# Attention pairs of one kind handled in joint steps, with the conversion of the first MLP's weights moved on the clock

## The chip, the cores and the metric

The kernel runs on one core of a Trainium2 chip. A core has five engines with instruction queues of their own, each worked off in order: PE (TensorE, matmuls), DVE (VectorE), ACT (ScalarE), POOL (GpSimd) and SP (SyncE, which issues the DMAs here). The metric is the device time of one execution in microseconds (us). Before the change it is 902.57 us, the median of three runs (900.73 to 903.84).

## The reference

Attention over 4 batches, 8 heads, 576 positions and a head width of 64, in fp32, then two MLPs over the 2304 tokens:

```python
scores = scale * np.matmul(q, k.transpose(0, 1, 3, 2))
mask_local = (rel >= 0) & (rel < 32)
mask_strided = (rel >= 0) & (pos[None, :] % 32 == pos[:, None] % 32)
scores = np.where(masks[None], scores, -1e9)      # heads 0-3 local, heads 4-7 strided
attn = np.exp(scores - scores.max(-1)); attn /= attn.sum(-1) + 1e-9
x = np.matmul(attn, v)                             # to (2304, 512)
h = x @ w_in;  x = (h * np.cos(h)) @ w_out         # 512 -> 2048 -> 512
g = x @ w_gate; x = (g * sigmoid(g) * (x @ w_val)) @ w_out2   # 512 -> 1536 -> 512
```

The kernel takes q, k, v and the results in float32 and the weights in float64, whose words it converts on the chip.

## The kernel before

**Attention (lines 321 to 455 and 622 to 709).** Two heads share the 128 partitions as a pair: 4 batches by 4 pairs, of which two are local (windows of 64 queries by 96 keys) and two strided (the positions of one residue modulo 32 stand together, three residues to a block of 54 by 54). A pair is cut into three groups of three local or four (last three) strided tiles. One step k of the loop at line 661 starts one group of a strided pair and the same group of a local pair, so that 8 runs of two pairs by 3 groups make 24 steps. A group is worked on over six steps: masks and scores on PE and the row maxima on DVE in its own step, exponentials on ACT one step later, row sums and a reciprocal on DVE and the division on POOL (`norm`, line 408) two steps later (LAGS[0]), transposes on PE and their copies out of PSUM on ACT three steps later, the product with v on PE four steps later, and the store into the token tile on ACT (`put`, line 442) five steps later. Each of these is one instruction (or a few) per group, so twice per step. Buffers turn: 4 score or scratch banks of PSUM, 2 transposed banks, 2 output banks, 3 tiles of q and k and of v per kind.

**The loads.** SP issues them in program order: q and k of a run (`load_qk`, 592 or 594 KB a pair), v (432 KB local, 2 by 162 KB strided), and 512 KB chunks of the weights (`load_raw`, six buffers). A chunk's buffer is loaded again as soon as the DVE instruction that reads it last has been issued. On POOL, `scale_q` multiplies the q of the next run by 1/8 in each middle group's step; it waits for that run's load.

**The filler.** Work on the weights is a queue of small pieces, each with a cost in us of DVE time (`later`, line 176). `pump(share)` adds a credit and takes pieces until it is spent; it is called twice in an attention step, with PUMP = 1.0 from step KP = 4 on. In order: for each of the 16 chunks of w_in a conversion to fp32 (`conv_steps`, line 197: ACT line 221, DVE lines 224, 228 and 232: scan for the maximum, shift, combine); from chunk XSAT = 12 on also the scale and the fp16 split of the first token block (lines 457 to 480); the common scale of w_in (lines 114 to 135); then for each chunk the split into two fp16 parts (`split_chain`, line 260: ACT line 242, DVE line 245), with the scan of one chunk of w_out (line 171) behind each. `need(key)` takes pieces until the one with that key is done, whatever the credit.

**First MLP (lines 833 to 889).** 80 slots: 5 token blocks by 16 hidden tiles. In a slot PE does the up projection of one tile (12 matmuls of up to 512 columns, line 503, "up1"), DVE, ACT and POOL make h*cos(h) of earlier tiles (DVE lines 519 and 526: two instructions a slot), and from slot HEAD = 14 on PE also does the down projections of tiles whose turn it is, as many as keep the queue of finished tiles at the length `lag`, which falls from HEAD - 2 to 2 by RATE = 0.4 a slot. Slot 0 is run inside the attention loop, at step 25, behind `need(("in", 0))`; the rest follow after step 29. The second load, conversion and split of w_out (`direct_later`, line 291) is filler again, and a down projection of tile m first takes pieces until w_out's chunk m is split. A PSUM bank of an up projection is free when DVE's second instruction has read it; up to slot HEAD - 5 every second projection uses one of four further banks. The weights of the second MLP are scanned, converted and written out behind that, with budgets of HSHARE, SHARE and SHARE2 of the DVE time that PE's work leaves.

Of the kernel before, what the change touches and what calls it, by code (L numbers as in the profile page):

```python
# [51 lines left out]
PUMP, KP = 1.0, 4  # L52
XSAT = 12
EARLY, K0 = 1, 1
HEAD, HSHARE = 14, 0.8
# [5 lines left out]
SHARE, SHARE2, SB = 0.95, 0.7, 2  # L61
# [14 lines left out]
def build(tc, qk_l, qk_s, v_l, v_s, w_in, w_out, w_gate, w_val, w_out2, mask_l, mask_s, eye32, eye16, out):  # L76
    nc = tc.nc
    wide = w_in.dtype != F32
    with ExitStack() as ctx:
# [117 lines left out]
        def conv_steps(mat, j, dst, scan, free=load_raw):  # L197
# [38 lines left out]
            return box, [(0, g0)] + [(0.63, g1)] * scan + [(0.36, g2), (0.63, g3)]  # L236
# [20 lines left out]
        def chain_later(mat, j, tiles):  # L257
            begin(conv_steps(mat, j, lambda: as_f32(tiles[j + 2]), True)[1])
# [65 lines left out]
        pa = attn.enter_context(tc.tile_pool(name="pa", bufs=2, space=bass.MemoryType.PSUM))  # L324
# [15 lines left out]

        units = [(b, p) for b in range(NB) for p in (2, 0, 3, 1)]
        qk_t, v_t = {}, {}

        def load_qk(i):
            b, p = units[i]
            loc = is_local(p)
            qk_t[i] = ap.tile([128, QKW[loc]], F32, name="qkl" if loc else "qks", bufs=3)
            nc.sync.dma_start(out=qk_t[i], in_=(qk_l if loc else qk_s)[b, p % 2])

        def load_v(i):  # L350
            b, p = units[i]
            loc = is_local(p)
            if loc:
                v_t[i] = ap.tile([LW, LT, 128], F32, name="vl", bufs=3)
                nc.sync.dma_start(out=v_t[i], in_=v_l[b, p % 2])
            else:
                v_t[i] = v_pair[i // 2 % 3]
                for u in range(2):
                    nc.sync.dma_start(out=v_t[i][64 * u:64 * u + SW, SP * u:SP * u + SP, :], in_=v_s[b, p % 2, u])
# [4 lines left out]
        def scale_q(i):  # L364
            q = qk_t[i][:, 0:S if is_local(units[i][1]) else QP]
            nc.gpsimd.tensor_scalar(out=q, in0=q, scalar1=SCALE, scalar2=1.0, op0=ALU.mult, op1=ALU.mult)

        class Group:
            def __init__(self, i, g):
                self.i, self.g = i, g  # L370
                self.b, self.p = units[i]
                self.loc = is_local(self.p)
                self.i0, self.n = groups(self.p)[g]
                self.w = LW if self.loc else SW

            def mask(self):
                n, w = self.n, self.w
                b = bank()
                self.sc = b[:, 0:n * w].rearrange("p (n w) -> p n w", w=w)
                mask = (ml[:, 0:3] if self.g == 0 else ml[:, 1:4]) if self.loc else ms[:, 0:n]  # L380
                nc.tensor.matmul(out=self.sc, lhsT=id16, rhs=mask, start=True, stop=False)
                nc.tensor.matmul(out=b[:, 288:512], lhsT=ones16, rhs=hot[:, 0:224], start=False, stop=False)

            def scores(self):
                for i in range(self.n):
                    q0 = (64 if self.loc else SW) * (self.i0 + i)
                    k0 = (S if self.loc else QP) + q0
                    for h in range(2):
                        r = slice(64 * h, 64 * h + 64)
                        nc.tensor.matmul(out=self.sc[r, i, :], lhsT=qk_t[self.i][r, q0:q0 + 64],  # L390
                                         rhs=qk_t[self.i][r, k0:k0 + self.w], start=False, stop=i == self.n - 1)

            def top(self):
                self.mx = ap.tile([128, 4], F32, name="mx", bufs=3)
                m = self.mx[:, 0:self.n]
                nc.vector.tensor_reduce(out=m, in_=self.sc, op=ALU.max, axis=AX.X, negate=True)

            def exps(self):
                self.t = (e_l if self.loc else e_s)[(self.i // 2 * 3 + self.g) % 4]
                self.e = self.t[:, 0:self.n, 0:self.w]  # L400
                for i in range(self.n):
                    nc.scalar.activation(out=self.e[:, i, :], in_=self.sc[:, i, :], func=AF.Exp, bias=self.mx[:, i:i + 1])

            def sums(self, ls):
                self.ls = ls
                nc.vector.tensor_reduce(out=self.ls[:, 0:self.n], in_=self.t[:, 0:self.n, 0:self.w + 1], op=ALU.add, axis=AX.X)

            def norm(self):
                nc.gpsimd.tensor_tensor(out=self.e, in0=self.e,
                                        in1=self.ls[:, 0:self.n].unsqueeze(2).to_broadcast([128, self.n, self.w]), op=ALU.mult)  # L410

            def transposes(self):
                if self.loc:
                    self.tp = pa.tile([128, self.n, 128], F32, name="tp")[0:LW]
                    for i in range(self.n):
# [237 lines left out]
        for i in range(2):  # L653
            scale_q(i)
# [419 lines left out]
```

## Time and profile before

| | |
|---|---|
| median of three runs | 902.57 us |
| profiled execution, its own time | 901.94 us |
| its span (first to last instruction) | 900.2 us |
| busy: PE, DVE, ACT, POOL | 857.6, 607.9, 490.9, 184.5 us |
| moved by DMA | 150.94 MB |

PE is busy for 95% of the span, but this is a mean over very different stretches. The profile's second part, 40 slices of 22.5 us, shows PE at six to eight tenths in the first five slices, with the DMA engines at nine tenths in the first three, and at nine tenths from there on. The attention loop and slot 0 take the first 122 us; what is left is nearly unbroken matmul work. Busy time of an engine is a sum over its instructions; what a stretch is limited by is read from what ends the idle time before them.

### The profile page before, as it was taken

The numbers are of one execution on the slowest core, as the hardware profiler recorded it, in microseconds if no ns is written. First come the engines' busy times: TensorE is split into PE (matmuls) and PEld (weight loads), VectorE is DVE, ScalarE is ACT, GpSimd is POOL, SyncE is SP. The second block draws the span as 40 slices with busy tenths as digits, with TensorE's granted clock in tenths as the row PEclk, the third lists the DMA queues.
The fourth block names the chain that finished last, engine by engine and source line by source line (L and its number), as shares of the span: only waits on it lengthen the run. The fifth ranks groups of instructions, "written<-read, shape, count | busy, mean of one in ns | idle before, by whom it ended". The sixth has DMA issues, their size and how long they took to land.

```text
span 900.2 us, 16865 instructions
## 1 busy us (share of the span) xinstructions
PE 857.6 (95%) x6687; PEld 561.1 (62%) x6687; DVE 607.9 (68%) x1138; ACT 490.9 (55%) x974; POOL 184.5 (20%) x223
## 2 busy tenths in 40 slices
PE   7678799999999999999999999999999999999997
PEld 5557544444444444555556777777777777888885
DVE  6678979887658989986687456554544554565444
ACT  4678878763435777654677334443434443443433
POOL 3344414212215666532222100000000000000000
PEclk9798999999999999999999999999999999999999
DMA  9998762357544565554243343343425334544501
GB/s 275 336 286 257 227 234 70 118 187 253 196 171 170 192 216 183 187 201 127 71 153 135 122 155 118 129 149 144 165 91 202 112 135 151 202 180 170 201 1 36
DMA packets 35391, 150.94 MB, mean 168 GB/s; under 512 B 4240, under 2 KB 5520, under 8 KB 31472
## 3 DMA queue, kind: packets, MB, share of 16 engines
q1 hardware_dynamic: 35312, 149.87, 48.9%
q8 instruction: 52, 0.85, 0.4%
q14 instruction: 27, 0.22, 0.1%
HBM read 134.13 MB, written 15.73 MB: 166 GB/s over the span
## 4 chain that ended last, share of the span: by engine, by line
PE 74%; DVE 10%; DMA 6%; ACT 4%; issue 3%; POOL 2%; ACTq 0%; POOLq 0%; SPq 0%; DVEq 0%
PE bank L483 14%; PE bank L485 14%; PE bank L484 14%; PE acc L484 11%; PE acc L485 11%; PE acc L483 11%; DMA raw<-w_in 6%; DVE cv L232 1%; ACT arena L242 1%; DVE arena L245 1%; DVE tb L526 1%; POOL arena L796 1%; DVE tb L519 1%; DMA v_pair<-v_s 1%; POOL arena L531 1%
## 5 line engine op out<-in xcount | busy, mean ns | idle before, releaser
L483 PE MATMUL bank<-xs,wi 128*128 128x256 f16 (+3 forms) x748 | 225.0, 301 | 10.4 <-DVE q L134 5.0
L485 PE MATMUL bank<-xs,wi 128*128 128x256 f16 (+3 forms) x748 | 224.8, 301 | 0.0
L484 PE MATMUL bank<-xs,wi 128*128 128x256 f16 (+3 forms) x748 | 224.8, 301 | 0.0
L483 PE MATMUL acc<-arena 128*128 128x512 f16 (+1 forms) x560 | 200.4, 358 | 1.0 <-ACT arena L605 1.0
L484 PE MATMUL acc<-arena 128*128 128x512 f16 (+1 forms) x560 | 200.4, 358 | 0.3 <-DVE arena L606 0.3
L485 PE MATMUL acc<-arena 128*128 128x512 f16 (+1 forms) x560 | 200.4, 358 | 0.0
L531 POOL TENSOR_TENSOR arena<-tb,arena 128x512 f16<-128x512 f32 (+1 forms) x80 | 91.2, 1142 | 239.0 <-ACT arena L530 211.0
L959 DVE TENSOR_TENSOR arena<-bank,cv 128x512 f32<-128x512 f32 (+1 forms) x90 | 57.2, 635 | 117.6 <-PE bank L485 117.6
L485 PEld LDWEIGHTS <-arena 128*128 128x128 f16 x952 | 93.2, 98 | 57.1 <-issue 0.5
L484 PEld LDWEIGHTS <-arena 128*128 128x128 f16 x952 | 93.2, 98 | 53.3 <-issue 1.2
L483 PEld LDWEIGHTS <-arena 128*128 128x128 f16 x952 | 93.2, 98 | 52.2
L484 PEld LDWEIGHTS <-wi 128*128 128x128 f16 x768 | 75.2, 98 | 50.4 <-issue 13.5
L484 PE MATMUL bank<-xs,arena 128*128 128x256 f16 (+1 forms) x392 | 102.4, 261 | 0.0
L485 PE MATMUL bank<-xs,arena 128*128 128x256 f16 (+1 forms) x392 | 102.4, 261 | 0.0
L483 PE MATMUL bank<-xs,arena 128*128 128x256 f16 (+1 forms) x392 | 102.4, 261 | 0.0
L483 PEld LDWEIGHTS <-wi 128*128 128x128 f16 x768 | 75.2, 98 | 39.2 <-issue 1.0
L485 PEld LDWEIGHTS <-wi 128*128 128x128 f16 x768 | 75.2, 98 | 34.4 <-issue 0.5
L605 ACT ACTIVATE arena<-tb 128x512 f16<-128x512 f32 (+1 forms) x60 | 35.2, 587 | 111.0 <-DVE tb L601 111.0
L516 ACT ACTIVATE tb<-bank,quarter,c 128x512 int32<-128x512 f32 (+1 forms) x75 | 54.3, 725 | 50.9 <-PE bank L485 41.8
L594 ACT ACTIVATE tb<-arena,c 128x512 f32<-128x512 f32 (+1 forms) x60 | 40.7, 679 | 66.4 <-DVE arena L959 65.4
L530 ACT ACTIVATE arena<-tb 128x512 f16<-128x512 f32 (+1 forms) x80 | 46.5, 581 | 40.9 <-PE acc L485 34.7
L600 DVE SCALAR_TENSOR_TENSOR tb<-tb,arena 128x512 f32<-128x512 f32 (+1 forms) x60 | 38.0, 633 | 38.8 <-ACT tb L594 38.8
(121 smaller groups left out, 1253.6 us busy)
## 6 DMA issues: line engine op xcount, KB each, us to landing
raw<-w_out SPq DMA_DIRECT2D x56, 512.0 KB
wi<-w SPq DMA_DIRECT2D x16, 1792.0 KB
arena<-w SPq DMA_DIRECT2D x14, 1792.0 KB
raw<-w_gate SPq DMA_DIRECT2D x24, 512.0 KB
raw<-w_val SPq DMA_DIRECT2D x24, 512.0 KB
w<-arena SPq DMA_DIRECT2D x42, 256.0 KB
raw<-w_in SPq DMA_DIRECT2D x16, 512.0 KB
qks<-qk_s SPq DMA_DIRECT2D x8, 594.0 KB
```

Source lines behind the costliest of these rows:

```text
L232: nc.vector.scalar_tensor_tensor(out=u, in0=box["l"], scalar=29, in1=u, op0=ALU.logical_shift_right, op1=ALU.bitwise_or)
L242: nc.scalar.activation(out=dst, in_=src, func=AF.Copy, scale=s)
L483: nc.tensor.matmul(out=o, lhsT=w[:, 0, c], rhs=x[0], start=first, stop=False, **kw)
L484: nc.tensor.matmul(out=o, lhsT=w[:, 0, c], rhs=x[1], start=False, stop=False, **kw)
L485: nc.tensor.matmul(out=o, lhsT=w[:, 1, c], rhs=x[0], start=False, stop=last, **kw)
L516: nc.scalar.activation(out=c["w"].bitcast(I32), in_=c["ph"], func=AF.Identity, scale=turn[c["blk"]], bias=quarter)
L530: nc.scalar.activation(out=g[:, 0, 0:n], in_=w, func=AF.Copy)
L531: nc.gpsimd.tensor_tensor(out=g[:, 1, 0:n], in0=w, in1=g[:, 0, 0:n], op=ALU.subtract)
L594: nc.scalar.activation(out=t, in_=c["C"][m][:, 0, 0:n], func=AF.Tanh, scale=half[c["blk"]])
L600: nc.vector.scalar_tensor_tensor(out=t, in0=t, scalar=1.0, in1=gate, op0=ALU.add, op1=ALU.mult)
L605: nc.scalar.activation(out=g[:, 0, 0:n], in_=t, func=AF.Copy)
L959: nc.vector.tensor_tensor(out=c["C"][m][:, :, h * right:h * right + h], in0=p, in1=t, op=ALU.add)
```

## The change

A step now starts one group of *both* pairs of one kind. Runs alternate local and strided, so there are again 8 runs by 3 groups. The scores of the two pairs stand in two neighbouring PSUM banks, and one instruction makes the maxima, the sums, the reciprocals, the division and the store of both. The scores have two buffers of two banks; transposes and outputs now come from the general pool of four banks. The two sets of exponentials have two buffers per kind instead of four, the zero-padded v of the strided pairs one buffer instead of three, and the loads follow the new order. In the filler, w_in's scan counts 0.9 instead of 0.63 (`PACE`), an attention step gives 0.8 twice instead of 1.0 twice, and a step after the last group (24 to 29) 1.2 twice (`TAIL`). The first token block's scale and split come behind chunk 5 instead of 12. The scans of w_out no longer alternate with the split of w_in but follow it. The first down projection comes at slot 18 or later instead of 14, with budgets of 0.85 and 0.78 for 0.8 and 0.7.

```diff
-PUMP, KP = 1.0, 4
-XSAT = 12
+PUMP, KP, PACE, TAIL = 0.8, 4, 0.9, 1.2
+XSAT = 5
-HEAD, HSHARE = 14, 0.8
+HEAD, HSHARE = 18, 0.85
-SHARE, SHARE2, SB = 0.95, 0.7, 2
+SHARE, SHARE2, SB = 0.95, 0.78, 2
...
-            return box, [(0, g0)] + [(0.63, g1)] * scan + [(0.36, g2), (0.63, g3)]
+            return box, [(0, g0)] + [(pace, g1)] * scan + [(0.36, g2), (0.63, g3)]
...
-        units = [(b, p) for b in range(NB) for p in (2, 0, 3, 1)]
+        runs = [(b, loc) for b in range(NB) for loc in (True, False)]
...
+        def score_banks():
+            return pa.tile([128, 2, 512], F32, name="sc", bufs=2)
...
+            def tops(self):
+                self.mx = ap.tile([128, 2, 4], F32, name="mx", bufs=3)
+                nc.vector.tensor_reduce(out=self.mx[:, :, 0:self.n], in_=self.sc, op=ALU.max, axis=AX.X, negate=True)
...
+                self.t = (e_l if self.loc else e_s)[self.g % 2]
...
+            def sums(self):
+                n = self.n
+                ls = ap.tile([128, 8], F32, name="ls", bufs=3)[:, 0:2 * n]
+                self.ls = ls.rearrange("p (u n) -> p u n", u=2)
+                nc.vector.tensor_reduce(out=self.ls, in_=self.t[:, :, 0:n, 0:self.w + 1], op=ALU.add, axis=AX.X)
+                nc.vector.reciprocal(out=ls, in_=ls)
             def norm(self):
                 nc.gpsimd.tensor_tensor(out=self.e, in0=self.e,
-                                        in1=self.ls[:, 0:self.n].unsqueeze(2).to_broadcast([128, self.n, self.w]), op=ALU.mult)
+                                        in1=self.ls.unsqueeze(3).to_broadcast([128, 2, self.n, self.w]), op=ALU.mult)
...
             def put(self):
+                p = 0 if self.loc else NPAIR // 2
+                dst = tokens[:, p:p + 2, S * self.b:S * self.b + S]
                 if self.loc:
+                    nc.scalar.activation(out=dst[:, :, 64 * self.i0:64 * (self.i0 + self.n)], in_=self.po, func=AF.Copy)
...
-        split_chain([("in", j, wi) for j in range(M1)], 2, lambda j: scan_later("out", j + 1) if j + 1 < M1 else top_later("out"))
+        split_chain([("in", j, wi) for j in range(M1)], 2)
+        for j in range(1, M1):
+            scan_later("out", j)
+        top_later("out")
...
+            share = 0 if k < KP else PUMP if duo(0) else TAIL
...
-            pump(PUMP if k >= KP else 0)
+            pump(share)
...
-            if pair(0) and g == 1 and i + 2 < len(units):
-                scale_q(i + 2)
-                scale_q(i + 3)
+            if g == 1 and i + 1 < len(runs):
+                scale_q(i + 1, 0)
+                scale_q(i + 1, 1)
...
+            if g == 2 and i + 3 < len(runs):
+                load_qk(i + 3, 0)
+                load_qk(i + 3, 1)
```

Three places show how the order of the instructions moves. The first is the load queue (SP) behind the first run's q and k and the constants; "raw" is a chunk buffer, "qks" and "qkl" (now "qk") are q and k. Before:

```order
L348 DMA qks<-qk_s 128x1188
L348 DMA qkl<-qk_l 128x1184
L359 DMA v_pair_107<-v_s 54x768 x2
L355 DMA vl<-v_l 96x1152
L162 DMA raw<-w_in 128x1024 x2
L359 DMA v_pair_108<-v_s 54x768 x2
L355 DMA vl<-v_l 96x1152
L162 DMA raw<-w_in 128x1024
L348 DMA qks<-qk_s 128x1188
L162 DMA raw<-w_in 128x1024
L348 DMA qkl<-qk_l 128x1184
L162 DMA raw<-w_in 128x1024 x2
```

And after:

```order
L347 DMA qk<-qk_s 128x1188 x2
L354 DMA vl<-v_l 96x1152 x2
L162 DMA raw<-w_in 128x1024 x2
L359 DMA vs<-v_s 54x768 x4
L347 DMA qk<-qk_l 128x1184 x2
L162 DMA raw<-w_in 128x1024 x2
L354 DMA vl<-v_l 96x1152 x2
L162 DMA raw<-w_in 128x1024 x2
L347 DMA qk<-qk_s 128x1188 x2
L162 DMA raw<-w_in 128x1024 x2
```

The third run's q and k now stand ahead of the third chunk of w_in, and the fourth run's ahead of the seventh.

The second place is ACT between the first instruction on slot 0's projection and the first on slot 1's; "wi" is w_in's split, "xy" a store of attention's result. Before, seen from the third of the last six groups on:

```order
L451 ACTIVATE xy<-po 128x12x18
L447 ACTIVATE xy<-po 128x192
L427 ACTIVATE pts<-tp 128x256
L427 ACTIVATE pt<-tp 96x384
L242 ACTIVATE wi<-wi,s_1604 128x512
L451 ACTIVATE xy<-po 128x12x18
L447 ACTIVATE xy<-po 128x192
L242 ACTIVATE wi<-wi,s_1604 128x512 x2
L451 ACTIVATE xy<-po 128x8x18
L447 ACTIVATE xy<-po 128x192
L242 ACTIVATE wi<-wi,s_1604 128x512 x3
L516 ACTIVATE tb<-acc_2035,quarter,c_1889 128x512
```

And after, the whole stretch:

```order
L523 ACTIVATE tb<-bank,quarter,c_1648 128x512
L433 ACTIVATE pt<-bank 128x256 x2
L458 ACTIVATE xy<-bank 128x2x12x18
L433 ACTIVATE pt<-bank 128x256 x2
L458 ACTIVATE xy<-bank 128x2x12x18
L242 ACTIVATE wi<-wi,s_1640 128x512 x4
L458 ACTIVATE xy<-bank 128x2x8x18
L242 ACTIVATE wi<-wi,s_1640 128x512 x7
L523 ACTIVATE tb<-acc_1774,quarter,c_1648 128x512
```

Between the two, 11 splits stand now where 8 stood (6 in the rows shown, two ahead of them), and two more that followed later stand ahead of slot 0's instruction.

The third place is DVE around the maximum of w_out ("pw_out") and the first split chunk of w_out ("arena<-cv"). Before, the maximum is formed in slot 3, with the split not before slot 7:

```order
L117 TENSOR_REDUCE m<-pw_out 128x1
L120 TENSOR_SCALAR a<-m 128x1
L122 SCALAR_TENSOR_TENSOR p<-m,a 128x1
L127 TENSOR_SCALAR tops<-id_72,p 128x128
L519 SCALAR_TENSOR_TENSOR tb<-acc_2078,c_1889,tb 128x512
L228 TENSOR_SCALAR cv<-cv 128x512
L526 SCALAR_TENSOR_TENSOR tb<-tb,bank 128x512
L232 SCALAR_TENSOR_TENSOR cv<-raw,cv 128x512
L519 SCALAR_TENSOR_TENSOR tb<-bank,c_1889,tb 128x512
```

And after, in slots 18 and 19:

```order
L117 TENSOR_REDUCE m<-pw_out 128x1
L120 TENSOR_SCALAR a<-m 128x1
L122 SCALAR_TENSOR_TENSOR p<-m,a 128x1
L127 TENSOR_SCALAR tops<-id_72,p 128x128
L228 TENSOR_SCALAR cv<-cv 128x512
L232 SCALAR_TENSOR_TENSOR cv<-raw,cv 128x512
L134 TENSOR_REDUCE q<-bank 128x1
L109 RECIPROCAL s_2249<-q 128x1
L110 TENSOR_SCALAR inv_2250<-q 128x1
L111 TENSOR_SCALAR s_2249<-s_2249 128x1
L228 TENSOR_SCALAR cv<-cv 128x512
L245 SCALAR_TENSOR_TENSOR arena<-cv,s_2249,arena 128x512
```

The maximum, the scale, the first conversion and its split now stand together, right ahead of the first down projection, which is in slot 19 (in slot 15 before).

## Rows read from the trace of the kernel before

**Rows 1.** Stretches: start:end, us, busy us (count) by engine, PEclk, DMA share, GB/s

```profile
20.00:36.00 16.00, 7.82 (x115) 6.37 (x116) 8.30 (x22) 7.68 (x26) 4.06 (x6) 0.68 1.02 355
36.00:46.00 10.00, 9.72 (x189) 7.94 (x187) 9.83 (x24) 8.85 (x32) 5.56 (x8) 1.00 0.99 286
...
88.00:104.00 16.00, 13.14 (x253) 10.66 (x252) 14.97 (x40) 13.38 (x47) 6.23 (x10) 1.00 0.76 221
...
122.00:155.00 33.00, 33.00 (x156) 15.05 (x155) 31.72 (x59) 28.38 (x45) 10.48 (x10) 1.00 0.40 139
```

**Rows 2.** Waits, 8 to 112 us: engine, line, releaser: total us, times, longest us

```profile
ACT wi L221 <- DMA raw<-w_in: 12.1, 5, 4.8
...
POOL qks L366 <- DMA qks<-qk_s: 9.8, 2, 8.2
```

**Rows 3.** PE's timeline: start us, us, instruction, count; L420 opens a step

```profile
35.73 0.44 PE L420 MATMUL tp<-id,e_s 128*128 128x128 f32 x2
...
41.94 0.44 PE L420 MATMUL tp<-id,e_s 128*128 128x128 f32 x2
...
102.86 0.44 PE L420 MATMUL tp<-id,e_s 128*128 128x128 f32 x2 [0.89 <-POOL e_s L409]
...
104.72 0.67 PE L390 MATMUL bank<-qkl 64*64 64x96 f32 x12
...
111.40 0.63 PE L483 MATMUL bank<-xs,wi 128*128 128x512 f16 x1
...
121.81 0.38 PE L483 MATMUL acc<-xs,wi 128*128 128x512 f16 x1 [0.48 <-ACT xy L447]
```

**Rows 4.** PE's waits from 121 to 219.5 us, as in rows 2

```profile
PE bank L483 <- DVE tb L526: 2.7, 3, 1.4
```

**Rows 5.** The chain of waits in order of time: start us, us, what

```profile
11.44 13.30 DMA raw<-w_in
```

**Rows 6.** DMA issues: count, KB each

```profile
raw<-w_in SPq DMA_DIRECT2D x16, 512.0 KB
qks<-qk_s SPq DMA_DIRECT2D x8, 594.0 KB
...
vl<-v_l SPq DMA_DIRECT2D x8, 432.0 KB
...
v_pair<-v_s SPq DMA_DIRECT2D x16, 162.0 KB
```

**Rows 7.** Groups by form, DVE, 0 to 122 us: busy us, mean ns, idle before

```profile
L232 DVE SCALAR_TENSOR_TENSOR wi<-raw,wi 128x512 int32<-128x512 int32 x16 | 12.4, 773 | 0.3
L396 DVE TENSOR_REDUCE mx<-bank 128x3 f32<-128x288 f32 x24 | 10.8, 450 | 10.3 <-ACT e_s L402 9.3 <-PE bank L390 0.6 <-ACT e_l L402 0.3
...
L224 DVE TENSOR_REDUCE pw_in<-raw 128x1 f32<-128x512 f32 x16 | 10.6, 664 | 0.0
...
L228 DVE TENSOR_SCALAR wi<-wi 128x512 int32<-128x512 int32 x16 | 7.0, 441 | 1.3 <-ACT wi L221 1.3
```

**Rows 8.** DVE's and POOL's timeline around 86 us, columns as in rows 3

```profile
85.75 0.94 DVE L232 SCALAR_TENSOR_TENSOR wi<-raw,wi 128x512 int32<-128x512 int32 x1
...
86.10 1.11 POOL L409 TENSOR_TENSOR e_l<-e_l,ls 128x288 f32<-128x288 f32 x1
```

**Rows 9.** DVE's timeline in the slots, columns as in rows 3

```profile
125.31 0.73 DVE L519 SCALAR_TENSOR_TENSOR tb<-bank,c,tb 128x512 f32<-128x512 f32 x1
...
161.99 0.74 DVE L519 SCALAR_TENSOR_TENSOR tb<-bank,c,tb 128x512 f32<-128x512 f32 x1
...
181.28 0.69 DVE L232 SCALAR_TENSOR_TENSOR cv<-raw,cv 128x512 int32<-128x512 int32 x1
...
183.43 0.68 DVE L232 SCALAR_TENSOR_TENSOR cv<-raw,cv 128x512 int32<-128x512 int32 x1
...
200.20 0.74 DVE L519 SCALAR_TENSOR_TENSOR tb<-bank,c,tb 128x512 f32<-128x512 f32 x1
```

More of the change, by code (lines that the diff above doesn't have):

```diff
@@ L195, in need, with conv_steps @@
                 step_fill()
-        def conv_steps(mat, j, dst, scan, free=load_raw):
+        def conv_steps(mat, j, dst, scan, free=load_raw, pace=0.63):
             part = parts_w[mat][:, j:j + 1]
@@ L342, in build, with load_qk @@
         qk_t, v_t = {}, {}
[L344 to L348, printed above, removed]
+        def load_qk(i, u):
+            b, loc = runs[i]
+            if not u:
+                qk_t[i] = ap.tile([128, 2, max(QKW.values())], F32, name="qk", bufs=3)
+            nc.sync.dma_start(out=qk_t[i][:, u, 0:QKW[loc]], in_=(qk_l if loc else qk_s)[b, u])
@@ L350, in load_v @@
         def load_v(i):
-            b, p = units[i]
-            loc = is_local(p)
+            b, loc = runs[i]
             if loc:
-                v_t[i] = ap.tile([LW, LT, 128], F32, name="vl", bufs=3)
-                nc.sync.dma_start(out=v_t[i], in_=v_l[b, p % 2])
+                v_t[i] = ap.tile([LW, 2, LT, 128], F32, name="vl")
+                for u in range(2):
+                    nc.sync.dma_start(out=v_t[i][:, u], in_=v_l[b, u])
             else:
-                v_t[i] = v_pair[i // 2 % 3]
+                v_t[i] = v_pads
@@ L358, in load_v, with scale_q @@
                 for u in range(2):
-                    nc.sync.dma_start(out=v_t[i][64 * u:64 * u + SW, SP * u:SP * u + SP, :], in_=v_s[b, p % 2, u])
+                    for r in range(2):
+                        nc.sync.dma_start(out=v_pads[64 * r:64 * r + SW, u, SP * r:SP * r + SP, :], in_=v_s[b, u, r])
         def bank():
             return pm.tile([128, 512], F32, name="bank")
-        def scale_q(i):
-            q = qk_t[i][:, 0:S if is_local(units[i][1]) else QP]
+        def scale_q(i, u):
+            q = qk_t[i][:, u, 0:S if runs[i][1] else QP]
@@ L384, in scores @@
             def scores(self):
[L385 to L396, printed above, removed]
-            def exps(self):
[L399 to L402, printed above, removed]
@@ L404, in sums @@
-            def sums(self, ls):
-                self.ls = ls
-                nc.vector.tensor_reduce(out=self.ls[:, 0:self.n], in_=self.t[:, 0:self.n, 0:self.w + 1], op=ALU.add, axis=AX.X)
+                for u in range(2):
+                    qk = qk_t[self.i][:, u]
+                    for i in range(self.n):
+                        q0 = (64 if self.loc else SW) * (self.i0 + i)
+                        k0 = (S if self.loc else QP) + q0
+                        for h in range(2):
+                            r = slice(64 * h, 64 * h + 64)
+                            nc.tensor.matmul(out=self.sc[r, u, i, :], lhsT=qk[r, q0:q0 + 64], rhs=qk[r, k0:k0 + self.w],
+                                             start=False, stop=i == self.n - 1)
@@ L433, in values @@
[L433 to L440 removed]
+                po = bank()
@@ new lines, in values @@
+                self.po = po[:, 0:2 * self.n * qn].rearrange("p (u n) -> p u n", u=2)
+                for u in range(2):
+                    for i in range(self.n):
+                        half = 0 if self.loc else 64 * (i % 2)
+                        at = 128 * (i if self.loc else i // 2)
+                        t = self.i0 + i
+                        t = t if self.loc else t % 2 * SP + t // 2
+                        for h in range(2):
+                            c = slice(64 * h, 64 * h + 64)
+                            nc.tensor.matmul(out=self.po[c, u, i * qn:i * qn + qn], lhsT=v_t[self.i][0:r, u, t, c],
+                                             rhs=self.pt[0:r, u, at + 64 * h:at + 64 * h + qn], start=True, stop=True)
```

173 lines of the change are left out of this document (75 added, 98 removed).

## The prediction

> **What bounds the kernel now.** I began with the stretches [rows 1]. From 122 us on PE is busy without a gap: 155 weight loads, one to a matmul, in 33.00 us, so a projection of 12 matmuls takes 2.56 us. From 121 to 219.5 us PE loses only 2.7 us to DVE [rows 4]. So the end is set by when the slots start, by the matmuls behind that (the change leaves them alone), and by what PE waits for in the slots. Before 122 us PE is not the bound. From 20 to 46 us the DMA share is 0.99 to 1.02 [rows 1], ACT waits 12.1 us for chunks of w_in and POOL 8.2 us in one piece for q [rows 2]: that is the load queue. From 88 to 104 us the DMA share is 0.76, and DVE is busy for 14.97 of 16 us: that is DVE.
>
> PE's timeline gives the pace [rows 3]. Where neither holds it, two steps take 41.94 - 35.73 = 6.21 us, 3.1 each: PE's own work of a step. From 41.94 to 102.86 us there are 14 steps, of 4.35 us each. Scores end at 104.72 + 0.67 = 105.4, slot 0's projection opens at 111.40 (call it S0) and slot 1's (S1) at 121.81.
>
> **The change part by part.** I sum to one point: PE has done 26 projections and 11 down projections after S1, 37 x 2.56 = 94.7 us of matmuls. In the profiled execution that is 121.81 + 94.7 + 2.7 = 219.2 us of its 900.2 us span. There, slot 27 in the changed kernel, its DVE has just worked off the pieces that it postponed. Later waits I take as unchanged: filler resumes with scans in both, DVE has slack there, and only the two smaller budgets differ (bounds 2 us either way).
>
> *Loads.* The third chunk of w_in lands at 11.44 + 13.30 = 24.74 us [rows 5]. In the new order the q and k of the fourth run stand behind four more loads of q and k, two of v_l and three chunks than that chunk did: 4 x 594 + 2 x 432 + 3 x 512 = 4776 KB [rows 6], 4.89 MB. At 355 GB/s until 36 us (4.0 MB) and 286 after that [rows 1] they land at 39.1. With POOL's multiplication by 1/8 and the division queued behind it (some 2 us together, an estimate from one division's 1.11 [rows 8]) step 9 opens at about 41, near the 41.94 of before. Bounds: 3 us either way, for what the 16 queues move ahead of it.
>
> *A step from there.* Before, DVE's attention part is a maximum and a sum for each kind, about 0.45 each for a local group [rows 7] and less for a strided one, with a reciprocal some 1.8 us; a filler credit of 2.0 buys 2.0 / 1.62 units of 0.66 + 0.44 + 0.77 = 1.88 [rows 7], 2.3 us. Together 4.1, against the measured 4.35. After, a maximum over 576 elements costs, on the line from 288 elements (0.450) to 512 (0.664) [rows 7], 0.72; over 432 0.59. Twice that and a reciprocal of 0.2 is about 1.5. The filler's nominal cost of a unit is now 1.89, its true one, so 1.6 buys 1.6 us. DVE: 3.1. PE: 3.1, as measured. ACT: its share of [rows 1] is 13.38 / 16 of a step of 4.35, 3.6; less joint stores (0.2) and fewer chunks (0.3) 3.1. Three engines stand at the same figure, with two score buffers in place of three or four, so some of each waits for another: I take 3.35. The floor is PE's 3.1; the ceiling is the 4.07 of before's late steps, which follow from 14.97 us of DVE in 16. Fourteen steps: 46.9, and 1.4 for the first block's common scale, which now falls among them. Step 23 opens at 89.3, its scores end 2.3 later: **91.6** against 105.4.
>
> *From there to S0.* Before, 6.0 us. Now the conversion must still finish: sums of the last two groups 1.6, five pieces of conversion 2.8 and a last unit 1.7 (by the lengths of [rows 7]), the chain of maxima and scale, a scan of w_out in it, 2.8 (short instructions that the rows don't show singly; between 2 and 4), the first split 0.7, hand-offs 1.1: 10.7, so **S0 = 102.3** (bounds 8 and 13).
>
> *S0 to S1.* Before 10.4. Scans no longer stand between the splits on DVE, but PE still passes five keep-warm steps, whose stores wait in ACT behind splits: I take 8 (bounds 6 and 10.4).
>
> *The slots.* The scans come here. DVE's first instruction on slot 0 stands behind 12 splits and the projection's 4.2 us. A split takes DVE 0.66 where nothing else waits, and before it went at 10.4 / 8 = 1.3 with a scan beside each; I take 0.9: S0 + 15.1. Then 18 slots hold 65 long instructions of 0.655, two shifts and four scale chains of 0.95, 47.2 us summed. The same sum for before's slots 1 to 14 is 34.1, where 161.99 - 125.31 = 36.7 went by [rows 9]: a factor of 1.076, so 50.8. The first chunk of w_out is split at S0 + 65.9. PE gets to the down projection that needs it after S1 and 19 projections: S0 + 8 + 48.7 = 56.7. **PE stands for 9.2 us.** From there the unit of conversion and split sets the pace, 183.43 - 181.28 = 2.15 [rows 9], with a wait for ACT in each that the rows of the slot work share: DVE's slots 19 to 25 sum to 44.5, by before's slots 15 to 19 (36.9 summed, 200.20 - 161.99 = 38.2) 46.1. PE's own work there is 46.0, so nothing is regained: slot 27 opens at S0 + 112.0.
>
> *Sum.* 102.3 + 112.0 = 214.3 against 219.2: 4.9 us less. Span 895.3; with the 1.7 us that lie around it, 897.0; the profiled execution (901.94) is 0.6 below the median, so **897.5**. S0 = 107.2 is the point of no gain.
>
> *Edits at nothing.* The single strided v buffer: its load waits in SP for the previous run's last product, but it is needed four steps, 13 us, later; SP's queue, raw chunks and q and k among it, stands for up to a step. If that cover is gone it costs 3 us a run, three times. What remains to be loaded at 39 us, 16 x (512 + 594 + 162) + 8 x 432 KB, 24.3 MB, less the 12.1 moved by then, are 12.2 MB [rows 6], 43 us at 286 GB/s against my 50: covered, narrowly. The clock: 0.68 was granted where PE idled between 20 and 36 us [rows 1]; a PE that stands for 9 us at slot 19 may meet a lower level, 1 to 2 us.
>
> *A rule against the change.* At 85.75 us DVE's combine of two SBUF inputs runs beside a division of 1.11 us on POOL and takes 0.94 [rows 8], against 0.69 in the slots [rows 9]: 0.25 lost. The Trainium skill, page "SBUF — State Buffer", section "Who interferes with whom", says that a DVE instruction with two SBUF inputs contends with a GpSimd instruction that reads SBUF, and that the later of two contenders fully blocks until the first is done. By that rule the joint division, one piece of twice the length, could hold a combine for its whole length; even at the 1.11 us of this one in every step the sum would be 14 x 0.9 = 12 us higher. The row shows a partial hold only, and my sum goes by the row.
>
> **Rivals.** *A, faster.* The loads don't hold the early steps, and steps run at PE's 3.1: 14 x 0.25 = 3.5 less, 2 from the loads, 2 from a shorter end: S0 = 94.8, time 890. For it: 3.1 was reached at 36 to 42 us with conversion running. Against: ACT and DVE have no slack at that pace.
>
> *B, slower: POOL's joint division holds DVE.* Each step has one division over two pairs. Before, 0.25 us was lost to one of half the size. If it holds DVE for most of the 1.11 us that a division takes [rows 8], a step is DVE's 3.1 plus 0.9 to 1.0, and stays at before's late 4.07: 14 x 0.72 = 10.1 later, S0 = 112.4, time 907.6. It decides from a step of 3.7 on (S0 = 107.2). For it: 0.94 and 1.11 at 85.75; against: the total length of the divisions doesn't grow.
>
> *C, no change: the loads set the pace, not DVE.* Six steps (two runs) need 4 x 594 KB of q and k, 2 x 432 + 4 x 162 of v and five chunks, 6.6 MB with the new queue kept full, 22.9 us at 286 GB/s: 3.8 a step, S0 = 108.6, time 903.8; with a few steps fed from what landed early, 902. Then the joint instructions save time that nothing waits for. Against: six buffers of chunks run ahead, so the average need is lower.
>
> **How the numbers follow.** Under 0.3%, 2.7 us, a measurement can't tell from no change. Forecast 0.40 (893 to 901, of which 0.03 within 0.3%), A 0.20 (886 to 893), C 0.20 (0.17 within, 0.03 slower), B 0.20 (905 to 912). Faster 0.57, same 0.20, slower 0.23. The range runs from 886 to 908: it takes in A and C, and half of B; its ends also hold the bounds of the step (3.1: -3.5, 4.07: +10) and of the way to S0. The forecast's own range is 893 to 901.
>
> **What would show it.** Right: steps of 3.2 to 3.5 from 41 us on, scores done near 92, S0 near 102, PE standing 7 to 12 us between slots 18 and 20 with DVE as releaser, slot 27 near 214. Wrong: steps of 3.7 or more with DVE's combines at 0.9 and over (B) or with waits of ACT and POOL on DMA beyond 60 us (C); S0 under 97 (A); PE standing for w_out's chunks beyond slot 27, which would say that the postponed scans cost more than the attention gave.

## The result and the profile after

The change makes the kernel slower by a little: 915.39 us, the median of four runs, against 903.21 for the kernel before in the same comparison; the ratio is 1.013, with a 95% interval of 1.0095 to 1.0165. The profiled execution took 915.56 us at a span of 913.7, 13.5 us more than before. The prediction was 897.5 us, with a range from 886 to 908.

The loss is not where the attention loop ends. Slot 0 and slot 1 open earlier than before, and PE's timeline of the changed kernel (columns as in [rows 3], which it answers to) shows by how little:

```profile
41.47 0.86 PE L426 MATMUL bank<-id,e_l 128*96 128x128 f32 x6 [1.02 <-POOL e_l L418]
...
54.45 0.66 PE L426 MATMUL bank<-id,e_s 128*128 128x128 f32 x4
...
61.48 0.47 PE L447 MATMUL bank<-pt,vs 118*64 118x54 f32 x4 [4.79 <-DMA vs<-v_s]
...
65.91 1.12 PE L426 MATMUL bank<-id,e_s 128*128 128x128 f32 x4
...
71.53 0.86 PE L426 MATMUL bank<-id,e_l 128*96 128x128 f32 x6
...
96.91 0.86 PE L426 MATMUL bank<-id,e_l 128*96 128x128 f32 x6
...
98.03 0.91 PE L395 MATMUL sc<-qk 64*64 64x54 f32 x24
...
107.69 0.29 PE L133 MATMUL bank<-tops,ones 128*128 128x128 bf16 x1 [4.84 <-DVE tops L127]
109.62 0.61 PE L490 MATMUL bank<-xs,wi 128*128 128x512 f16 x1 [1.65 <-ACT wi L242]
...
120.02 0.38 PE L490 MATMUL acc<-xs,wi 128*128 128x512 f16 x1
```

Step 9 opens at 41.47, step 23 at 96.91. Two of these fourteen steps are long: the one from 54.45 to 65.91 waits for the strided pairs' v, and the one behind it takes 5.6 us. The other twelve take 38.4 us, 3.2 each. The scores end at 98.9 (105.4 before), but slot 0's projection, at 109.62, is only 1.8 us ahead of before, and so is slot 1's.

The same stretches as in [rows 1], of the changed kernel (the third and fourth were chosen for the wait):

```profile
20.00:36.00 16.00, 9.07 (x136) 7.64 (x134) 6.73 (x15) 7.57 (x29) 4.07 (x5) 0.68 1.02 298
36.00:46.00 10.00, 8.98 (x186) 7.86 (x183) 8.09 (x15) 9.02 (x28) 3.76 (x4) 1.00 1.04 328
46.00:60.00 14.00, 10.14 (x201) 8.64 (x197) 10.91 (x28) 11.66 (x42) 6.92 (x8) 1.00 0.96 270
60.00:66.00 6.00, 2.75 (x33) 2.16 (x34) 1.24 (x3) 0.00 (x0) 1.48 (x1) 0.57 1.03 261
...
88.00:104.00 16.00, 13.71 (x281) 11.76 (x279) 14.58 (x29) 15.27 (x54) 5.86 (x6) 1.00 0.55 179
104.00:122.00 18.00, 12.35 (x119) 6.43 (x120) 8.09 (x21) 7.36 (x14) 0.73 (x1) 0.72 0.34 114
122.00:155.00 33.00, 30.16 (x134) 13.26 (x133) 30.46 (x54) 27.17 (x43) 9.30 (x9) 0.95 0.34 111
```

The columns are PE, PEld (weight loads), DVE, ACT and POOL. From 60 to 66 us ACT does nothing, PE is busy for 2.75 us, DVE and POOL for 1.2 and 1.5, while the DMA share is 1.03. From 104 to 122 us DVE is busy for 8.1 of 18 us, ahead of a stretch in which PE waits for it: 133 weight loads in 33 us stand against 155 before [rows 1].

Behind slot 1 PE waits far more. Its waits from 120.5 us to the end of the span (columns as in [rows 2]), of the changed kernel:

```profile
PE bank L490 <- DVE q L134: 7.4, 7, 2.8
PE bank L490 <- DVE tb L533: 6.5, 5, 1.7
PE bank L133 <- DVE tops L127: 2.8, 1, 2.8
PE acc L490 <- ACT arena L242: 2.8, 1, 2.8
PE acc L490 <- ACT arena L612: 1.0, 1, 1.0
...
```

And of the kernel before, from 121 us on:

```profile
PE bank L483 <- DVE q L134: 5.0, 7, 1.7
PE bank L483 <- DVE tb L526: 4.9, 5, 1.5
PE acc L483 <- ACT arena L605: 1.0, 1, 1.0
...
```

To place the loss I use one measure for all kernels below, the **lag**: the time from slot 1's opening until PE has issued so many us of matmuls (columns at the 0.2155 us that 512 of them take in the timeline), less those matmuls. It holds PE's waits and what a lower clock costs. At 94.7 us of matmuls, the point to which the prediction sums, the lag is 3.8 us before and 11.8 after; at 450 us, past the last of the first MLP's waits, 14.7 and 29.3. So the change gains 1.8 us up to slot 1, loses 8.0 in the first slots and 6.6 more behind them: 12.8 of the 13.5.

### The profile page after: what moved, and what is told of

It reads as the page before. It is cut to its first block, busy times and chain, and to the rows that moved or that the text cites. A ratio compares the mean times of both kernels' runs of the same rounds, so it can differ in the third digit from the quotient of the medians.

```text
span 913.7 us, 16631 instructions
## 1 busy us (share of the span) xinstructions
PE 861.3 (94%) x6687; PEld 564.2 (62%) x6687; DVE 600.1 (66%) x1088; ACT 490.7 (54%) x950; POOL 174.2 (19%) x193
## 4 chain that ended last, share of the span: by engine, by line
PE 72%; DVE 8%; DMA 7%; ACT 5%; POOL 4%; issue 3%; POOLq 0%; DVEq 0%; ACTq 0%
PE bank L490 13%; PE bank L492 13%; PE bank L491 13%; PE acc L491 10%; PE acc L490 10%; PE acc L492 10%; POOL arena L538 2%; DMA qk<-qk_l 2%; DMA raw<-w_in 2%; DVE arena L245 1%; POOL arena L801 1%; DMA vs<-v_s 1%; PE bank L447 1%; DVE tb L533 1%; PE sc L395 1%
## 5 line engine op out<-in xcount | busy, mean ns | idle before, releaser
L964 DVE TENSOR_TENSOR arena<-bank,cv 128x512 f32<-128x512 f32 (+1 forms) x90 | 57.2, 636 | 118.6 <-PE bank L492 118.5
```

What stands on the lines that cost most here:

```text
L964: nc.vector.tensor_tensor(out=c["C"][m][:, :, h * right:h * right + h], in0=p, in1=t, op=ALU.add)
```

## The experiments

Fourteen kernels ran, with 4 to 10 runs each, against the kernel before in the same comparison. Since the kernel before had medians of 899.5 to 903.2 in the five comparisons, the ratio is the figure to compare. S0, S1 and the lags are from one profiled execution of each kernel, which took up to 4.6 us more than the median (e11) and up to 2.6 less (e10).

| kernel | S0 | S1 | lag at 94.7 | lag at 450 | median us | ratio (interval) |
|---|---|---|---|---|---|---|
| before | 111.4 | 121.8 | 3.8 | 14.7 | 903.21 | 1 |
| the change | 109.6 | 120.0 | 11.8 | 29.3 | 915.39 | 1.013 (1.0095 to 1.0165) |
| e1 | 101.3 | 111.0 | 10.6 | 28.1 | 904.26 | 1.0044 (1.0022 to 1.0065) |
| e2 | 103.6 | 113.9 | 11.7 | 29.3 | 906.65 | 1.0073 (1.0048 to 1.0097) |
| e3 | 108.2 | 118.5 | 13.2 | 34.0 | 917.47 | 1.0189 (1.0147 to 1.023) |
| e4 | 106.0 | 116.3 | 11.6 | 26.9 | 910.06 | 1.0102 (1.0066 to 1.0138) |
| e5 | 112.7 | 121.6 | 4.1 | 17.5 | 901.64 | 1.0012 (0.9992 to 1.0032) |
| e6 | 104.9 | 115.3 | 3.8 | 15.4 | 895.11 | 0.9935 (0.9917 to 0.9953) |
| e7 | 102.5 | 113.7 | 10.4 | 26.2 | 904.16 | 1.0036 (1.0012 to 1.0061) |
| e8 | 110.2 | 122.5 | 7.9 | 19.5 | 907.96 | 1.0086 (1.0058 to 1.0114) |
| e9 | 104.7 | 113.7 | 6.1 | 20.9 | 900.92 | 1.0003 (0.9988 to 1.0018) |
| e10 | 104.3 | 113.7 | 11.0 | 30.1 | 912.09 | 1.0133 (1.0103 to 1.0164) |
| e11 | 105.5 | 116.7 | 7.9 | 20.2 | 897.86 | 0.9976 (0.996 to 0.9992) |
| e12 | 104.9 | 113.8 | 4.1 | 21.5 | 900.4 | 1.0008 (0.9992 to 1.0024) |
| e13 | 101.1 | 111.5 | 11.3 | 28.8 | 906.99 | 1.0079 (1.0057 to 1.0101) |
| e14 | 109.5 | 121.5 | 16.3 | 31.3 | 917.4 | 1.0186 (1.0164 to 1.0208) |

**The late load.** e1 leaves it out, e2 puts it ahead of other loads.

```diff
                 elif i > 1:
-                    load_v(i)
+                    v_t[i] = v_pads
```

> The changed kernel without the strided pairs' v loads of the second to fourth batch (it computes with the first batch's v there). Theory: the 10.7 us that PE stood between 54 and 67 us, waiting for that load, are what kept slot 0 late; without them slot 0 opens near 99 us instead of 109.6 and the time is about 905 us (903 to 908). Rival (the load queue as a whole is late, and w_in's chunks are next): slot 0 after 105 us and a time above 910.

Slot 0 opens at 101.3 us, 8.3 us earlier, slot 1 at 111.0; the lags stay within 1.2 us. The stand is what kept the slots late.

```diff
-            if g == 2 and i + 3 < len(runs):
-                load_qk(i + 3, 0)
-                load_qk(i + 3, 1)
-            if g == 0 and 2 <= i < len(runs):
-                if runs[i][1]:
-                    load_v(i + 2) if i + 2 < len(runs) else None
-                elif i > 1:
-                    load_v(i)
+            if g == 0 and 2 < i < len(runs) and not runs[i][1]:
+                load_v(i)
+            if g == 0 and 1 <= i and i + 2 < len(runs):
+                load_qk(i + 2, 0)
+                load_qk(i + 2, 1)
+            if g == 1 and 2 < i < len(runs) - 1 and not runs[i][1]:
+                load_v(i + 1)
```

> The changed kernel with the order of three loads changed: the strided v of a run ahead of the q and k of the run two later, and the local v of the next run one step behind that. 2.1 MB less stand ahead of the late load, 7 us at 290 GB/s. Theory (order): PE's stand at 54 to 67 us falls from 10.7 to about 3 us, slot 0 opens near 102, time 907 to 910. Rival (bandwidth): the stand moves to the loads that were put behind, q and k of the sixth run or chunks of w_in, and the time stays at 913 to 916.

Slot 0 opens at 103.6, the scores end at 93.1, and the time is just under the range that I expected. No data is moved less and no buffer added, so what was late was the load's place in the queue. SP's timeline of the changed kernel shows it (columns as in [rows 3]; the second figure runs from the first issue of a group to the end of its last):

```profile
40.88 2.44 SPq L347 DMA_DIRECT2D qk<-qk_s  x2
45.47 0.33 SPq L162 DMA_DIRECT2D raw<-w_in  x1
48.55 5.07 SPq L359 DMA_DIRECT2D vs<-v_s  x4
```

and the chain of waits, in order of time:

```profile
38.05 15.28 DMA raw<-w_in
53.33 0.02 issue
53.35 11.69 DMA vs<-v_s
```

The four loads were issued between 48.55 and 53.62 us, and the last of them landed at 65.04, 11.7 us after its issue, behind q and k of a run that needed them two steps later than v. The issue itself was held up too: from 40 to 66 us SP stands at L359 for 6.5 us until earlier transfers have landed, the last time for the chunk of w_in in the chain above, and for 0.2 us for PE, which frees the buffer. So it was not the wait for the single buffer. In the kernel of e6, which has the order of e2, SP's timeline has the same group in 1.65 us, and PE waits for it nowhere:

```profile
47.52 1.65 SPq L359 DMA_DIRECT2D vs<-v_s  x4
```

**The attention and the numbers apart.** e5 takes the change's attention with all of before's numbers, e6 is e5 with the load order of e2, e7 is the kernel before with the change's numbers (the edits of e5 the other way round).

```diff
-PUMP, KP, PACE, TAIL = 0.8, 4, 0.9, 1.2
-XSAT = 5
+PUMP, KP, PACE, TAIL = 1.0, 4, 0.63, 1.0
+XSAT = 12
-HEAD, HSHARE = 18, 0.85
+HEAD, HSHARE = 14, 0.8
-SHARE, SHARE2, SB = 0.95, 0.78, 2
+SHARE, SHARE2, SB = 0.95, 0.7, 2
-        split_chain([("in", j, wi) for j in range(M1)], 2)
-        for j in range(1, M1):
-            scan_later("out", j)
-        top_later("out")
+        split_chain([("in", j, wi) for j in range(M1)], 2, lambda j: scan_later("out", j + 1) if j + 1 < M1 else top_later("out"))
```

> The changed attention steps and loads alone: filler and slot numbers as before (PUMP 1.0, PACE 0.63, TAIL 1.0, XSAT 12, scans of w_out beside the split, HEAD 14, HSHARE 0.8, SHARE2 0.7). Theory (the loss behind slot 1 is DVE work that the new numbers leave for the slots): PE's waits behind slot 1 are as before (about 15 us by 587 us, not 29), steps of 3.8 us, slot 0 near 111 with the late v load, time 899 to 905. Rival (the joint instructions or the new buffers cause them): waits of 25 us or more, time above 909.

> As e5_joint_alone, with the strided v's load ahead of q and k as in e2_v_ahead_of_qk. Theory: slot 0 near 105, waits behind slot 1 as before, time 893 to 899, faster than both kernels. Rival (DVE is what the loop waits for with the old filler, so the late load hides): the same time as e5_joint_alone within 2 us.

> The kernel before with the change's filler and slot numbers alone (PUMP 0.8, PACE 0.9, TAIL 1.2, XSAT 5, scans of w_out behind the split, HEAD 18, HSHARE 0.85, SHARE2 0.78). Theory: the loop gets shorter (a step is 1.8 us of attention and 1.6 of filler on DVE; slot 0 near 105 in place of 111.4) and the slots lose 12 to 15 us: 905 to 912. Rival (the slots' loss needs the changed attention): waits behind slot 1 as before and a time of 895 to 899.

With before's numbers the lag is near that of before (17.5 and 15.4 against 14.7), with the change's numbers it is 26.2 even under the old attention (e7 opened slot 0 earlier than I expected, and its time is just under my range). So the changed attention doesn't cause it. As a whole it is a gain (joint instructions, buffers and the order of loads were not run apart): in e6 a step takes 3.99 us (step 9 at 42.33, step 23 at 98.19) against 4.35, and e6 is **faster than both kernels**, by 0.65% of the time before. The late load alone eats that gain: e5 is no different from before. And e7 shows that the short step is not due to the joint instructions: with the small credit the old steps take 3.40 us (41.32 to 88.92).

**The numbers one by one**, each put into e6 alone:

```diff
 e8: w_out's scans behind the split, as in the change
 e9: HEAD, HSHARE = 18, 0.85 and SHARE2 = 0.78
 e10: PUMP, KP, PACE, TAIL = 0.8, 4, 0.9, 1.2
 e11: PUMP, KP, PACE, TAIL = 1.0, 4, 0.75, 1.2
 e12: SHARE2 = 0.78
```

> e6_joint_v_ahead with w_out's scans behind the whole split of w_in, as in the change, and nothing else. Theory (what counts is how much DVE work is left for the slots, and the credit hands out the same amount): PE's waits behind slot 1 stay at 15 to 18 us, time 893 to 898. Rival (the order counts: the maximum of w_out comes too late for the first down projection at slot 14): waits of 22 us or more, time above 900.

> e6_joint_v_ahead with the change's slot numbers (HEAD 18, HSHARE 0.85, SHARE2 0.78) and nothing else. If the waits between 345 and 412 us come from these numbers by themselves (later opening, larger budget): 7 us more of them, time 900 to 904. If they come only with DVE work left over from the loop (theory): 893 to 898.

> e6_joint_v_ahead with the change's filler pace (PUMP 0.8, PACE 0.9, TAIL 1.2) and nothing else. Theory: steps of about 3.2 us, slot 0 near 102, so 3 us earlier than in e6_joint_v_ahead, but 10 us or more of DVE work moved into the slots, where PE waits 28 to 35 us: 904 to 912. Rival (slack on DVE in the slots takes it up): 890 to 894.

> e6_joint_v_ahead with a pace between the two (PUMP 1.0, PACE 0.75, TAIL 1.2). Theory: the loop gets 1 to 3 us shorter and the slots lose as much: 893 to 898, the same as e6_joint_v_ahead. Rival (the loss in the slots is a step, not in proportion): 888 to 892 or above 900.

> e6_joint_v_ahead with SHARE2 = 0.78 and nothing else (HEAD 14, HSHARE 0.8). If the larger budget is what makes PE wait for DVE between 337 and 383 us in e9_slot_numbers: those waits appear here too (5 us or more above e6_joint_v_ahead by 400 us), time 898 to 902. If the later opening behind HEAD = 18 is needed for them: waits as in e6_joint_v_ahead, 893 to 897.

e10 is the largest loss, and shows what the pace does. DVE's busy time up to slot 1, in e6 and in e10 (start:end, us, DVE busy (count), PEclk, DMA share, GB/s):

```profile
0.00:115.30 115.30, 89.75 (x172) 0.94 0.92 287
```

```profile
0.00:113.70 113.70, 76.74 (x155) 0.91 0.84 260
```

13.0 us of DVE's work are left for the slots, and slot 1 opens 1.6 us earlier. Even that is not the pace: in e9 and e12, whose attention is that of e6, slot 1 opens at 113.7 and 113.8 as in e10, and of these three only e6's profile shows a lower clock ahead of it (0.76 granted from 109 to 116 us, 1.00 in e9 and e12). The scores do end 7.2 us earlier in e10 (93.0 against 100.2), but slot 0 now waits until w_in is converted: 11.3 us from there, against 4.7 in e6, where the conversion is done by then. What is left over turns up as a lag of 30.1 instead of 15.4. e11, with part of the pace, loses in between; the rival that DVE's slack takes the work up, and the one of a step, fall.

e8 refuted me. I had held that only the amount of postponed work counts; DVE's busy time by slot 1 is the same (88.8 us, 89.8 in e6), yet slot 1 opens 7.2 us later. The rival that I had named, a late maximum of w_out, isn't it either: most of the loss lies ahead of slot 1. DVE's waits from 95 to 135 us in e8:

```profile
DVE wi L245 <- ACT wi L242: 10.8, 6, 4.2
DVE pw_out L171 <- DMA raw<-w_out: 4.6, 5, 1.8
```

and in e6:

```profile
DVE wi L245 <- ACT wi L242: 2.9, 3, 2.2
```

A split is ACT's instruction and then DVE's. ACT has attention's copies and stores in the same queue; where splits follow one another, ACT is full (busy for 7.73 us from 103 to 111 us in e8), and DVE, busy for 4.88, stands for it. A scan between two splits is DVE work that needs no ACT, and its end also starts the next load of w_out. Busy times of the stretch show the same, e6 and then e8 (columns as in [rows 1]):

```profile
95.00:135.00 40.00, 35.33 (x347) 20.45 (x346) 35.51 (x66) 33.88 (x74) 9.11 (x9) 0.96 0.68 230
```

```profile
95.00:135.00 40.00, 31.09 (x322) 18.77 (x323) 25.25 (x44) 25.72 (x61) 5.09 (x4) 0.87 0.37 137
```

e9 refuted me too: without any postponed work the slot numbers bring 5.5 us of lag by 450. e12 shows which of them: SHARE2 alone leaves the lag at 94.7 as it was and adds 5.8 behind it, from 11.6 to 17.4. PE's waits of e12 from 215 to 420 us:

```profile
PE bank L490 <- DVE q L134: 5.2, 3, 4.4
PE bank L490 <- DVE tb L533: 2.4, 4, 0.8
PE bank L133 <- DVE tb L533: 1.2, 1, 1.2
```

and of e6, where the longest is 2.4 us:

```profile
PE bank L490 <- DVE q L134: 3.5, 4, 2.4
PE bank L490 <- DVE tb L533: 2.3, 2, 1.5
```

My reading is that a larger credit puts more conversion ahead of the instructions on DVE that PE waits for; which instructions moved I did not follow. Part of the 5.8 is the clock: behind the wait of 4.4 us the granted clock is 0.50 from 321.5 to 328.3 us, where e6 has 1.00.

**Back inside the change.** e3 and e4 are made from the change, e13 and e14 from e2.

```diff
 e3:
-HEAD, HSHARE = 18, 0.85
+HEAD, HSHARE = 14, 0.8
 e3 and e4:
-SHARE, SHARE2, SB = 0.95, 0.78, 2
+SHARE, SHARE2, SB = 0.95, 0.7, 2
 e13:
-        split_chain([("in", j, wi) for j in range(M1)], 2)
-        for j in range(1, M1):
-            scan_later("out", j)
-        top_later("out")
+        split_chain([("in", j, wi) for j in range(M1)], 2, lambda j: scan_later("out", j + 1) if j + 1 < M1 else top_later("out"))
 e14:
-PUMP, KP, PACE, TAIL = 0.8, 4, 0.9, 1.2
-XSAT = 5
+PUMP, KP, PACE, TAIL = 1.0, 4, 0.63, 1.0
+XSAT = 12
```

> The changed kernel with the slot numbers of before (HEAD 14, HSHARE 0.8, SHARE2 0.7). Theory: the 7 us of PE's waits between 345 and 412 us come from the second MLP's conversion, which opens later behind HEAD = 18 and is pressed together; they go, while the waits up to 220 us (11.8 us) stay within 3 us: 906 to 910 us. Rival (they come from what the attention loop left undone): waits up to 220 us grow by the 4 slots that the first down projection comes earlier, and the time is 914 or more.

> The changed kernel with SHARE2 = 0.7 as before and HEAD = 18 kept. If the larger budget is what makes DVE late between 345 and 412 us: about 908 us, and those waits near 3 us. If the late opening is (theory): the same pieces are only spread to later slots, 913 to 916 us.

> e2_v_ahead_of_qk (the change with the v load ahead) with w_out's scans beside the split as before. Theory (the slow pace has left the scans for the slots whatever their order): 905 to 910, within 3 us of e2_v_ahead_of_qk. Rival (DVE's wait for ACT's part of the split is what the change loses): slot 1 opens 4 us or more earlier, or waits behind it fall by 5 us, and the time is 901 or less.

> e2_v_ahead_of_qk with the filler pace of before (PUMP 1.0, PACE 0.63, TAIL 1.0, XSAT 12), scans behind the split and slot numbers of the change kept. Theory (both order and pace cost; with this pace the splits come in the loop's tail, where DVE waits for ACT, as in e8_scans_behind): 904 to 910. If the pace is all: 899 to 902, as e9_slot_numbers.

My theory for e3 and e4, that the waits at 345 to 412 us come from the later opening behind HEAD = 18, is refuted. With SHARE2 alone taken back, e4 has 0.8 us of them left (6.2 in the change), as e12 had it from the other side. But 15.3 us of lag are still added between 94.7 and 450 (17.5 in the change): 4.0 us of PE's waits now stand at 513 to 555 us (0.8 in the change), in the second MLP, on copies by ACT and DVE. Its other gain is a slot 0 at 106.0, which isn't the edit's: it is the same attention program as the change's. e3 differs from e4 in HEAD and HSHARE alone and is 7.4 us slower, with 7.1 more lag at 450, so the later first down projection does help once work has been postponed. In e13 the order alone changes nothing beyond the noise (1.0079 against 1.0073), as the theory had it: with the slow pace most scans come in the slots either way. In e14 the old pace, with XSAT, makes things worse, by 1.1%, and misses both of my expectations: the splits then fall together in the loop's tail, DVE waits for ACT for 10.8 us as in e8, and one wait of PE for DVE in the slots is 6.65 us. The numbers don't add up one by one, and the way they combine was measured only in these four; XSAT, HEAD and HSHARE were never run alone.

## Why the prediction was wrong, step by step

**The late load was the first failure.** I put the single strided buffer among the edits at nothing, needed four steps, 13 us, after its issue, with 3 us a run if that failed. I had checked that all loads together fit the loop; that is no statement on one load's place. The cover was there and was too short once: issue to landing took up to 15.3 us (the chunk of w_in in the chain), in a stretch with a DMA share of about 1. The step from 54.45 was 8.3 us longer than 3.2, and the one behind it, at a granted clock of 0.54 from 65.91 to 71.53 us, 2.4: together 10.7 us. Slot 1 opened 9.7 us later than I forecast (120.0 against 110.3), and without that load 0.7 us later (111.0 in e1). Even so e1 is not faster than the kernel before (1.0044): the second failure, below, is needed to explain that. Its two later uses cost nothing: PE waits for v at no other place, and from 88 to 104 us the DMA share is 0.55.

**The loop itself was right.** Step 9 at 41.5 (41). Twelve steps at 3.2, and in e1 fourteen at 3.33 on average (41.95 to 88.53), where I took 3.35. (Two small sums of the prediction are off and change nothing: 12 x 0.9 + 4.2 is 15.0, not 15.1, and 6.6 MB at 286 GB/s take 23.1 us, not 22.9.) The rows of DVE's and POOL's groups of the changed kernel, 0 to 125 us (columns as in [rows 7]):

```profile
L232 DVE SCALAR_TENSOR_TENSOR wi<-raw,wi 128x512 int32<-128x512 int32 x16 | 13.0, 811 | 0.3
...
L400 DVE TENSOR_REDUCE mx<-sc 128x6 f32<-128x576 f32 x12 | 9.1, 755 | 19.0 <-PE sc L395 18.8
L414 DVE TENSOR_REDUCE ls<-e_l 128x6 f32<-128x582 f32 x12 | 9.0, 751 | 0.0
```

```profile
L418 POOL TENSOR_TENSOR e_l<-e_l,ls 128x576 f32<-128x576 f32 x12 | 14.1, 1176 | 28.0 <-DVE ls L415 16.4 <-ACT e_s L407 5.9 <-ACT pt L433 5.8
```

A joint maximum takes 0.755 us (I took 0.72). The joint division takes 1.18, and the combine beside it 0.81 in place of 0.77 [rows 7]: rival B, the division that holds DVE, cost 0.04 us an instruction, and fell. My ground against it was wrong, though. The row at 85.75 can't be read as a partial hold by the division of 1.11 us: that one began behind the combine, and another division had begun ahead of it, as POOL's timeline of the kernel before shows:

```profile
85.59 0.55 POOL L409 TENSOR_TENSOR e_s<-e_s,ls 128x216 f32<-128x216 f32 x1 [2.80 <-DVE ls L673]
```

In the changed kernel a combine just behind the start of a longer division takes 0.59 us more than its 0.69:

```profile
82.33 0.91 POOL L418 TENSOR_TENSOR e_s<-e_s,ls 128x432 f32<-128x432 f32 x1 [1.82 <-DVE ls L415]
```

```profile
82.52 1.28 DVE L232 SCALAR_TENSOR_TENSOR wi<-raw,wi 128x512 int32<-128x512 int32 x1
```

A combine came so soon behind a division twice in 16 (82.52 and 101.40). That it is so rare is what kept the cost small, and I had not worked that out: on this term the forecast was lucky. A and C fell as stated: the pace was as forecast, and the loads delayed one step, not all.

**The way to S0 was right, its size too:** 98.9 to 109.6 is the 10.7 us that I summed. What I had not drawn from it is that with the slow pace S0 is bound by w_in's conversion on DVE, not by the scores (PE's wait of 4.84 us ahead of 107.69): an attention loop that ends 7 us earlier because it does less filler (e10) brings slot 0 forward by 0.6. S0 to S1 took 10.4 as before, not 8, and DVE came to slot 0's first instruction at 127.57, S0 + 18.0, not 15.1: its waits for ACT's half of the split were 11.3 us between 95 and 135 us, 4.9 before. Most of that is one wait, in DVE's timeline and then ACT's:

```profile
119.91 2.96 DVE L245 SCALAR_TENSOR_TENSOR wi<-wi,s 128x512 f16<-128x512 f32 x4 [8.78 <-ACT wi L242]
```

```profile
114.95 0.78 ACT L523 ACTIVATE tb<-bank,quarter,c 128x512 int32<-128x512 f32 x1 [4.78 <-PE bank L492]
...
119.19 1.30 ACT L242 ACTIVATE wi<-wi,s 128x512 f16<-128x512 f32 x2
```

ACT works in order: its first instruction on slot 0 waits for the projection, which took 5.2 us at a granted clock of 0.50 (I took 4.2), then come attention's copies and stores, and only then the splits that DVE waits for. I had costed a split by DVE's pace, 0.9, and left ACT's queue out. The missing scans are not the cause here: with them back between the splits (e13) DVE still waits 8.4 us for ACT.

**In the slots the size was right and the place too narrow.** I forecast one stand of PE, 9.2 us, at the first down projection; the lag at 94.7 is 11.8. It comes in pieces. PE's timeline and two stretches of the changed kernel (columns as in [rows 3] and [rows 1]):

```profile
148.92 0.22 PE L133 MATMUL bank<-tops,ones 128*128 128x128 bf16 x1 [2.84 <-DVE tops L127]
...
177.00 0.61 PE L490 MATMUL acc<-arena 128*128 128x512 f16 x1 [2.81 <-ACT arena L242]
```

```profile
149.00:155.00 6.00, 6.00 (x22) 2.38 (x22) 5.97 (x14) 4.68 (x8) 2.32 (x2) 0.72 0.51 169
...
177.00:183.00 6.00, 6.00 (x21) 2.30 (x22) 3.85 (x8) 2.73 (x5) 0.80 (x1) 0.72 0.42 146
```

PE first waits 2.84 us at 148.92 for the second block's maxima (L127), a small product that I had not seen as a place where PE meets DVE in order, and 2.81 at 177.00 for the first split chunk of w_out. Behind each wait 21 or 22 matmuls go out in 6 us, 28 at full clock. These two waits, 1.7 us of clock behind each, and a wait of 1.7 at 219.97 make 10.8 of the 11.8. The first chunk was ready nearly when I had it, at S0 + 67.4 (65.9); but PE came to it at S0 + 64.6, not 56.7, since it had lost time on the way to slot 1 and at 148.92.

**The step that failed second is "later waits I take as unchanged", with bounds of 2 us.** From 94.7 to 450 us of matmuls the lag grows by 17.5, by 10.9 before: 6.6 us that I had bounded by 2. I had called SHARE2 one of "two smaller budgets" and given it no sum; put into e6 alone (e12) it adds 5.8 us there, taken out of the change (e4) it gives 2.2 back. The postponed work was not worked off by slot 27 either: the pace alone (e10) adds 7.5 us behind 94.7. How much of the 6.6 is due to each stays open, since the two don't add up.

Forecast to result, in spans: 895.3 to 913.7, 18.4 us. Slot 1 was 9.7 us late. From there to 94.7 us of matmuls I had forecast 6.6 us more than before (9.3 against 2.7), and the lag grew by 8.0 (3.8 to 11.8): 1.4. Behind that came 6.6, and past 450 us 0.7 (13.5 less 12.8): 18.4.

## What to carry to other kernels

Filler that an engine must do anyway is not saved by taking it out of a loop: look what the next stage waits for (here w_in's conversion, not the scores), and count what is left over against the slack behind it. Price a load that shares a queue by what stands ahead of it at its issue, not by the total; putting it ahead of loads that are needed later cost nothing here and decided between no gain and 0.65%. Pieces that pass from one engine to another want pieces of one engine between them where the first engine is full (e8; in e13 it made no difference).

## What the runs showed that I had not expected

A wait of PE of nearly 3 us can cost more than its length. At 149 to 155 and 177 to 183 us the granted clock is 0.72 of full speed on average, right behind waits of 2.84 and 2.81 us: 6 us x 0.28 = 1.7 us each. In the middle of it, from 150 to 153 us, it is 0.50, the lower of two levels (1.2 of 2.4 GHz). I had allowed 1 to 2 us for the whole. It isn't so each time: behind a wait of 2.67 us at 138.6 in e8 the granted clock is 1.00 (138 to 146 us).

Issuing itself can be slow: the same group of four loads took SP 5.07 us in the change, where it waited for earlier transfers to land, and 1.65 in e6.

The late load's cost varies: with the same attention program slot 0 opened at 109.6, 108.2 and 106.0 us in three kernels (the change, e3, e4), so a profile of one run can't size it to better than some 3 us.
